# First products of the MLP in half of its pieces as eleven block products instead of twelve, with block sums made in place

## The chip, the cores and the metric

The kernel runs on one core of a Trainium2 chip. The metric is device time in microseconds, from one launch. In the profile's rows the core's engines are PE (TensorE; PEld is its loading of weights), DVE (VectorE), ACT (ScalarE), POOL (GpSimd) and SP (SyncE, which here only issues DMAs). SBUF holds 128 partitions; PSUM has eight banks, each 512 fp32 columns wide, into which TensorE accumulates and from which ACT and DVE read.

## The reference

Attention with a delta rule over q, k, v of shape 4 x 8 x 768 x 48, then a two-layer MLP over 3072 tokens. All arithmetic is fp32; w_in and w_out arrive as 64-bit floats and are narrowed on the chip.

```python
k_n = k / (norm(k) + 1e-6)
for t in range(768):                         # per batch b and head h
    y[t] = q[t] @ state
    state += beta[t] * outer(k_n[t], v[t] - k_n[t] @ state)
x = y.transpose(0, 2, 1, 3).reshape(3072, 384)
h = x @ w_in                                 # 384 x 2048
out = (h * sigmoid(h)) @ w_out               # 2048 x 384
```

## The kernel before

**Tiling.** The 768 tokens of a sequence are worked in six chunks c = 0 to 5 of 128 tokens (of all four batches and eight heads), each in two halves hf of 64 tokens. A half is 256 rows of x (4 batches x 64 tokens), kept transposed as xT: 3 blocks k of 128 features, 256 columns. There are thus twelve MLP halves (c, hf).

**The MLP of a half.** `hidden(c, hf)` makes the first product in eight steps f. Each step covers 256 of the 2048 hidden features: six matmuls of a 128x128 weight by 256 columns (j = 0, 1 and k = 0 to 2) fill one bank `phid` (L952), and one ScalarE activation (L962, Silu) of 128x512 moves it into a tile `gT`, which holds three steps (a group). An fp32 matmul appears in the trace as two records, so that a half has 96 of them. `combine(c, hf)` makes the second product for c > 0. It is done with a scheme of seven products of blocks: seven chains of eight matmuls 128x128 by 192 columns (L1050), accumulated in the banks `px` and `py`. Their left operands are blocks of gT or sums S1 to S4 of such blocks, made by VectorE (`sum_g`, L1032) into `sums_of_g`; their right operands are blocks of w_out or the three sums `sums_of_w`, made once. Results go into `o` by ScalarE (scaled by 0.5); three of them are first kept by ScalarE (`kept`, L1058) and added by VectorE (L1061). In the last half of the program VectorE adds the last one straight from PSUM (L1096). For chunk 0 `project` makes the second product plainly (L982).

**The attention.** For each chunk `prepare` makes scores (`pg` L408, `pa` L488, copied by ScalarE at L503 and masked by VectorE at L498), writes them to DRAM in another layout (`blocks`) and reads them back (`g`). `invert` then inverts triangular 32x32 blocks with 31 steps of two VectorE operations (L562, L567) and ends at L570; its results travel through DRAM again (`up`, `xi`, `xe`), and `merge` (L711) joins them. `solve` uses the result: `keys` (ph, L757), `inner` (pz, L769), `update` (pu, L789), `old` and `new` (pyc, L835 and L848). `new` copies its output into xT; what lies on other partitions goes through `part` and is moved by DMAs (`move`, L828).

**Order.** Every instruction's place on its engine is fixed: `pin` ties each operation behind the last one on the same engine, and `in_line` does so for SyncE's DMAs. The MLP is a stream of generator steps (`pieces`); the attention code calls `run(n)` at fixed places, which executes the next n steps. So a hand-written order interleaves the two on every engine. In chunk c's part of the loop, `solve(c)` runs with the MLP's steps left over from the chunk before; `feed_forward(c, 0)` and `feed_forward(c, 1)` are added to the stream at its step n == 6; then follow `prepare(c + 1)` and `invert(c + 1)`, where three of four steps of the inversion also run a step of the MLP:

```python
for n, _ in enumerate(invert(c + 1, step)):
    if n % 4 != 3:
        run()
```

Banks come from three pools: A and CC for the attention, M for the MLP. In chunk 0 `joins` (33 to 59 us) uses A and CC for the first merge.

Of the kernel before, what the change touches and what calls it, by code (L numbers as in the profile page):

```python
# [19 lines left out]
def kernel(  # L20
# [10 lines left out]
    nc = tc.nc  # L31
# [24 lines left out]
    mlp = ctx.enter_context(tc.tile_pool(name="mlp", bufs=2))  # L56
    psA = ctx.enter_context(tc.tile_pool(name="psA", bufs=3, space=PSUM))
    psC = ctx.enter_context(tc.tile_pool(name="psC", bufs=3, space=PSUM))
    psM = ctx.enter_context(tc.tile_pool(name="psM", bufs=2, space=PSUM))
    A, CC, M = (psA, "a"), (psC, "c"), (psM, "m")  # L60
# [98 lines left out]
    def in_blocks(c):  # L159

        return 1 < c < NCH
# [27 lines left out]
    states = [const.tile([P, HB, NP, W], FP32, name=f"state{g}") for g in range(2)]  # L189
    beta_fm = mlp.tile([BH, NCH, 2, W], FP32, name="beta_fm", tag="gT", bufs=3)  # L190
    for g in range(2):
# [65 lines left out]
    def fetch_w_in(i):  # L257
        if i in (0, 1, 6):
            raw = mlp.tile([P, SIZE], U32, name="raw", tag="gT", bufs=3)[:]
        elif i < 6:  # L260
            raw = room(i // 2 - 1, i % 2)
        else:
            raw = spare
        raw = raw.rearrange("p (a f) -> p a f", a=NKT)
        src = moe_w_in.rearrange("(a p) f -> p a f", p=P)[:, :, i * WF : (i + 1) * WF].bitcast(U32)
        in_line(nc.sync.dma_start(out=raw, in_=src))
        raws["in", i] = raw.rearrange("p a (f j) -> p a f j", j=2)
# [495 lines left out]

    def inner(c, g, hf, room=A):

# [60 lines left out]
    def move():  # L826
        for to, of in moves:
            in_line(nc.sync.dma_start(out=to, in_=of))  # L828
        moves.clear()

# [12 lines left out]
    def new(c, g, hf):  # L843
# [13 lines left out]
        for h in chained(range(1, H, 2), range(0, H, 2)):  # L857
            f = D * h
            while f < D * (h + 1):
# [4 lines left out]
                if h % 2 == 1:  # L864
                    if g == 1:
                        moves.append((
                            xT[f % P : f % P + n, f // P].rearrange("p (g t) -> p g t", g=2),
                            parts[c, hf][at : at + n, :, h // 2, :],
                        ))
                else:  # L870
                    by_act(to, py[at : at + n, C * (h // 2) : C * (h // 2 + 1)])
# [71 lines left out]
    gTs = {}  # L943

    def hidden(c, hf):

        for f in range(NFF // 2):
            assert ("in", f) in narrowed
            ph = bank(M, "phid")
            for j in range(2):  # L950
                for a in range(NKT):
# [3 lines left out]
                        rhs=xTs[c, hf][:, a, :],  # L955
                        start=(a == 0), stop=(a == NKT - 1),
                    ))
                if j == 0:
                    yield
            if f % FG == 0:  # L960
                gTs[f // FG] = mlp.tile([P, FG, 2 * GT], FP32, name="gT", bufs=3)
            pin(nc.scalar.activation(  # L962
                out=gTs[f // FG][:, f % FG, :], in_=ph[:], func=ACTF.Silu, scale=-0.5 if in_blocks(c) else 0.5
            ))
            if c > 0 and f % FG == 1 and f >= FG:
                for which in (S1, S2):
                    sum_g(which, f // FG - 1)
            yield
# [32 lines left out]
    def sum_w():  # L1001
# [14 lines left out]
    S1, S2, S3, S4 = (  # L1016
        (0, (0, 1), (1, 1), ALU.add), (1, 0, (0, 0), ALU.subtract),
        (0, (0, 0), (0, 1), ALU.subtract), (1, (1, 0), 1, ALU.subtract),
    )
# [3 lines left out]

    def sum_g(which, g):
        k, left, right, op = which
        fs = group(g)
        of = [
            sums_of_g[:, x, fs] if isinstance(x, int) else
            gTs[g][:, 0 : fs.stop - fs.start, x[0] * GT + x[1] * C : x[0] * GT + (x[1] + 1) * C]
            for x in (left, right)  # L1030
        ]
        pin(nc.vector.tensor_tensor(out=sums_of_g[:, k, fs], in0=of[0], in1=of[1], op=op))  # L1032

    NG = -(-NFF // 2 // FG)

    def combine(c, hf):

        o = mlp.tile([P, 2, DM], FP32, name="o", bufs=1)
        kept = mlp.tile([P, 3, HM], FP32, name="kept", bufs=1)
        px, py = bank(M, "px"), bank(M, "py")  # L1040
        left, right = slice(0, HM), slice(HM, DM)
        last = c == NCH - 1 and hf == 1

        def chain(to, a, b, start=False):
            for f in range(NFF // 2):
                if isinstance(a, int):
                    at = sums_of_g[:, a, f]
                else:
                    at = gTs[f // FG][:, f % FG, a[0] * GT + a[1] * C : a[0] * GT + (a[1] + 1) * C]
                pin(nc.tensor.matmul(  # L1050
# [5 lines left out]

        def keep(i, of):
            pin(nc.scalar.mul(kept[:, i], of, 0.5))  # L1058

        def add(to, of):  # L1060
            pin(nc.vector.tensor_tensor(out=to, in0=to, in1=of, op=ALU.add))  # L1061

        def steps(chain, *halfway):
            for n, _ in enumerate(chain):
                if n == 1:
                    break
                for which, g in halfway:
                    sum_g(which, g)
                yield

        yield from steps(chain(px[:, left], (0, 0), (0, 0), True), (S1, NG - 1), (S2, NG - 1))
        yield
        yield from steps(chain(px[:, right], (1, 1), 2))
        pin(nc.scalar.mul(o[:, :, left], px[:, 0:DM].rearrange("p (n m) -> p n m", n=2), 0.5))
        yield
        yield from steps(chain(py[:, left], 0, (0, 1), True))
        pin(nc.scalar.mul(o[:, 1, right], py[:, left], 0.5))
        yield
        yield from steps(chain(px[:, left], 1, 1), *((S3, g) for g in range(NG)))
        pin(nc.scalar.mul(o[:, 0, right], px[:, left], 0.5))  # L1080
        yield
        yield from steps(chain(py[:, right], (1, 0), (1, 0)), *((S4, g) for g in range(NG)))
        keep(0, py[:, right])
        if last:
            add(o[:, 0, left], kept[:, 0])
            store(c, hf, o, 0, left)
        yield
        yield from steps(chain(px[:, left], 0, 0))
        keep(1, px[:, left])
        add(o[:, 1].rearrange("p (n m) -> p n m", n=2), kept[:, 1].unsqueeze(1).to_broadcast([P, 2, HM]))  # L1090
        if last:
            store(c, hf, o, 1)
        yield
        yield from steps(chain(py[:, left], 1, (1, 1)))
        if last:
            pin(nc.vector.scalar_tensor_tensor(  # L1096
                out=o[:, 0, right], in0=py[:, left], scalar=0.5, in1=o[:, 0, right], op0=ALU.mult, op1=ALU.add
            ))
            store(c, hf, o, 0, right, True)
            yield  # L1100
            return
        keep(2, py[:, left])
        add(o[:, 0, right], kept[:, 2])
        add(o[:, 0, left], kept[:, 0])
        for n in range(2):
            store(c, hf, o, n)
        yield

    def feed_forward(c, hf):

        yield from hidden(c, hf)
        if c > 0:
# [293 lines left out]
    for c in range(1, NCH):  # L1406
        solving = solve(c)
        long = lengths(c + 1) if c + 1 < NCH else iter(())
        for n in range(10):
            go(solving)  # L1410
            run(2 if n == 6 else 0 if n == 5 and c == 1 else 1)
            if n == 6:
                if c == 1:
                    run(999)
                    needed = iter(())
                pieces = chained(pieces, feed_forward(c, 0), feed_forward(c, 1))
            go(long, (1, 1, 0, 1, 1, 9, 5, 5, 5, 5)[n])
# [51 lines left out]
```

## Time and profile before

| | us |
|---|---|
| runs | 674.14, 676.48, 677.03 |
| median | 676.48 |
| profiled execution | 676.0 |
| its span | 674.3 |
| PE busy, its granted clock | 647.6, 0.984 |
| ACT busy | 218.6 |
| POOL busy | 84.3 |

The profiled execution is 1.7 us longer than the span of its instructions and 0.5 us below the median. A row of the page reads: line, engine, operation, output<-inputs, shape, count | busy time, mean ns of one | idle time of the engine just before these instructions, and what ended most of it. Matmuls are pipelined: a record's duration is longer than the spacing of records. A row of the chain or the timeline reads: start, duration, engine, group of instructions.

### The profile page before, as it was taken

How to read it: one execution, taken by the hardware profiler on the slowest of the kernel's cores; microseconds unless marked ns; L12 is line 12 of the kernel's file. 1: busy time of each engine (PE TensorE's matmuls, PEld its weight loads, DVE VectorE, ACT ScalarE, POOL GpSimd, SP SyncE). 2: the span in 40 equal slices, each digit the busy share in tenths (PEclk: the TensorE clock that was granted, in tenths of full speed). 3: DMA queues.
4: the chain of work that ended last, by engine and by line, in shares of the span. 5: the costliest groups of instructions: out<-in, count | busy, mean ns of one | idle time of the engine just before them, and what ended most of it. 6: DMA issues, size and time to landing. Idle time of an engine off the chain costs nothing.

```text
span 674.3 us, 20956 instructions
## 1 busy us (share of the span) xinstructions
PE 647.6 (96%) x9288; PEld 566.1 (84%) x9288; DVE 388.4 (58%) x883; ACT 218.6 (32%) x504; POOL 84.3 (13%) x86
## 2 busy tenths in 40 slices
PE   8849998899999999999999999999999999999997
PEld 5548885586688989988989988989888989989997
DVE  5846687994463892573982574973564972312112
ACT  2436675022343122443122442122442132431111
POOL 5022384400102000102000002001002000000000
PEclk9967999999999999999999999999999999999999
DMA  9891628505072904076814076624073023010101
GB/s 131 207 265 61 216 97 178 102 0 107 10 154 46 153 23 96 13 125 129 110 35 85 15 141 128 90 50 72 15 154 76 1 70 50 17 36 1 24 0 24
DMA packets 146906, 55.72 MB, mean 83 GB/s; under 512 B 118192, under 2 KB 139952, under 8 KB 146816
## 3 DMA queue, kind: packets, MB, share of 16 engines
q1 hardware_dynamic: 144624, 54.07, 40.7%
q8 instruction: 73, 1.20, 0.8%
q10 hardware_dynamic: 2192, 0.31, 0.3%
q14 instruction: 17, 0.14, 0.1%
HBM read 40.40 MB, written 11.80 MB: 77 GB/s over the span
## 4 chain that ended last, share of the span: by engine, by line
PE 75%; DVE 4%; DMA 3%; ACT 1%; issue 1%; SPq 1%; POOL 0%; ACTq 0%; DVEq 0%
PE phid L952 31%; PE px L1050 15%; PE py L1050 12%; PE po L982 4%; PE pa L488 2%; PE pz L769 2%; PE pu L789 2%; PE px L711 2%; PE py L711 2%; PE ph L757 2%; PE pyc L835 1%; PE pyc L848 1%; DVE rank L562 1%; DMA sums_of_w<-in_moe_w_out_dram 1%; DVE x L567 1%
## 5 line engine op out<-in xcount | busy, mean ns | idle before, releaser
L952 PE MATMUL phid<-xT,w_in 128*128 128x256 f32 x1152 | 257.2, 382 | 0.0
L952 PEld LDWEIGHTS phid<-xT,w_in 128*128 128x128 f32 x1152 | 216.3, 190 | 31.4 <-issue 1.9
L962 ACT ACTIVATE gT<-phid 128x512 f32<-128x512 f32 x96 | 57.4, 598 | 159.3 <-PE phid L952 153.1
L1032 DVE TENSOR_TENSOR sums_of_g<-gT 128x384 f32<-128x384 f32 (+1 forms) x60 | 29.2, 509 | 79.8 <-ACT gT L962 69.5
L562 DVE SCALAR_TENSOR_TENSOR rank<-g,step,x 128x31 f32<-128x31 f32 (+15 forms) x155 | 63.8, 412 | 17.7 <-DMA g<-blocks 13.2
L1050 PE MATMUL py<-w_out,sums_of_g 128*128 128x192 f32 x320 | 58.2, 331 | 0.0
L567 DVE TENSOR_TENSOR x<-x,rank 128x31 f32<-128x31 f32 (+15 forms) x155 | 54.7, 353 | 5.4
L1050 PE MATMUL px<-sums_of_w,sums_of_g 128*128 128x192 f32 x320 | 57.2, 330 | 0.0
L1050 PEld LDWEIGHTS px<-sums_of_w,sums_of_g 128*128 128x128 f32 x320 | 52.0, 190 | 0.8
L1050 PEld LDWEIGHTS py<-w_out,sums_of_g 128*128 128x128 f32 x320 | 51.9, 190 | 0.8
L982 PE MATMUL po<-w_out,gT 128*128 128x384 f32 x128 | 44.3, 495 | 5.1 <-POOL w_out L221 2.5
L351 POOL TENSOR_TENSOR sq<-kb 128x384 f32<-128x384 f32 x24 | 21.1, 898 | 223.4 <-PE px L711 217.4
L982 PEld LDWEIGHTS po<-w_out,gT 128*128 128x128 f32 x128 | 23.4, 190 | 20.9 <-POOL w_out L221 3.1
L450 DVE STREAM_TRANSPOSE kq<-stage 128x512 f32<-128x512 f32 x28 | 28.5, 1101 | 11.6 <-DMA stage<-in_q_dram 9.1
L503 ACT COPY xT<-pyc 48x128 f32<-48x128 f32 x132 | 34.2, 259 | 1.7
L769 PEld LDWEIGHTS pz<-vf,xi 64*64 64x64 f32 x768 | 27.4, 141 | 6.2 <-issue 4.8
L430 POOL TENSOR_TENSOR vf<-vf,n_slot 128x768 f32<-128x768 f32 x10 | 15.6, 1577 | 129.7 <-DMA vf<-in_v_dram 97.2
L769 PE MATMUL pz<-vf,xi 64*64 64x48 f32 x768 | 30.3, 227 | 1.3 <-issue 1.2
L498 DVE TENSOR_TENSOR ap<-pa,above 128x256 f32<-128x256 f32 x44 | 16.6, 419 | 22.8 <-ACT ap L503 21.8
L1061 DVE TENSOR_TENSOR o<-o,kept 128x192 f32<-128x192 f32 (+1 forms) x29 | 11.5, 421 | 31.5 <-ACT kept L1058 31.3
L1050 PE MATMUL py<-w_out,gT 128*128 128x192 f32 x160 | 29.1, 331 | 0.0
L1050 PE MATMUL px<-w_out,gT 128*128 128x192 f32 x160 | 27.6, 326 | 0.0
(172 smaller groups left out, 855.6 us busy)
## 6 DMA issues: line engine op xcount, KB each, us to landing
vf<-in_v_dram SPq DMA_DIRECT2D x24, 192.0 KB, 4.6
out_dram<-o SPq DMA_DIRECT2D x46, 96.0 KB, 2.2
sums_of_w<-in_moe_w_out_dram SPq DMA_DIRECT2D x5, 768.0 KB, 5.9
w_out<-in_moe_w_in_dram SPq DMA_DIRECT2D x4, 768.0 KB, 7.1
blocks<-ap SPq DMA_DIRECT2D x44, 64.0 KB, 1.9
g<-blocks SPq DMA_DIRECT2D x5, 512.0 KB, 3.6
up<-x SPq DMA_DIRECT2D x5, 512.0 KB, 4.0
xi<-up SPq DMA_DIRECT2D x20, 128.0 KB, 3.9
```

What stands on the lines that cost most here:

```text
L351: pin(nc.gpsimd.tensor_tensor(out=squared[c, b // HB][:, b % HB], in0=kb, in1=kb, op=ALU.mult))
L450: pin(nc.vector.transpose(out=kqs[c, b][:, :, j, :].rearrange("p a (i m) -> p a m i", i=T), in_=src.rearrange("p a (m d) -> p a m d", d=D) ...
L503: return pin(nc.scalar.copy(to, of))
L562: pin(nc.vector.scalar_tensor_tensor(out=tv, in0=g[:, 0:m, m : m + 1].to_broadcast([P, m, n]), scalar=step[:, m : m + 1], in1=x[:, m : m + ...
L567: yield pin(nc.vector.tensor_tensor(out=x[:, 0:m, m:T], in0=x[:, 0:m, m:T], in1=tv, op=ALU.add))
L711: yield pin(nc.tensor.matmul(pm[to, T * n : T * (n + 1)], lhsT=left, rhs=right, start=True, stop=True))
L769: yield pin(nc.tensor.matmul(pz[rows, n * D : (n + 1) * D], lhsT=xis[g][rows, u * H + 2 * p + e, :], rhs=vfs[c][rows, hf, g * HB + u, p, : ...
L952: pin(nc.tensor.matmul(ph[:, j * GT : (j + 1) * GT], lhsT=w_in[:, a, (2 * f + j) * P : (2 * f + j + 1) * P], rhs=xTs[c, hf][:, a, :], star ...
L962: pin(nc.scalar.activation(out=gTs[f // FG][:, f % FG, :], in_=ph[:], func=ACTF.Silu, scale=-0.5 if in_blocks(c) else 0.5))
L982: pin(nc.tensor.matmul(po[n][:, 0:DM], lhsT=gTs[f // 2 // FG][:, f // 2 % FG, at : at + C], rhs=w_outs[f // HFF][:, f % HFF, :], start=(f ...
L1032: pin(nc.vector.tensor_tensor(out=sums_of_g[:, k, fs], in0=of[0], in1=of[1], op=op))
L1050: pin(nc.tensor.matmul(to, lhsT=at, rhs=quarter(f, *b) if isinstance(b, tuple) else sums_of_w[b][:, f], start=start and f == 0, stop=f == ...
```

## The change

Six of the twelve halves, `FAST`, make the first product differently: (1,0), (2,0), (3,0), (4,0), (5,0) and (5,1). There `hidden_fast` treats the two weight columns i, the two halves n of the 256 columns and the blocks k = 0 and 1 as a product of 2x2 blocks, which needs seven block products in place of eight; k = 2 adds four plain ones. That is eleven matmuls of 128x128 by 128 columns per f instead of six by 256, which are twelve such blocks.

The scheme needs sums of weight blocks, s1 to s4 for each f, made once by GpSimd (`supply`: six f's in chunk 1 at n == 6, the others later); sums of x, t3, t2, t4 and one in place in xT, made by GpSimd at the start of each FAST half; and partial results, which are copied out of the bank by ScalarE (`begin_pair`: 128x256, `sixth`: 128x128, `seventh`: 128x128), added by VectorE (128x128 and, from PSUM, 128x384) and then activated (128x128 and 128x384). sixth and seventh write the same quarter of the bank, one after the other has been copied away.

All of gT is now one buffer, `gbuf`, which also takes the weights' and x's sums. The sums S1 to S4 are made in place in gT, for every half. So they must wait for the matmuls that read what they overwrite: S1 of the first two groups stays in hidden, S2 moves into combine, and S3 and S4 come later in it. px and py are added into o by VectorE straight from PSUM where the next half is FAST, and otherwise through ScalarE's copy, which now also holds for the last half of the program. `ahead_of_time` starts the next half, where it is FAST, within the combine before it (three of its steps). `late` marks (5,0), whose next half is FAST as well: there S4 is made in another block. The banks are A 2, CC 2, M 4, where they were 3, 3, 2; `inner` uses CC. Staging of beta and of some raw w_in moves into gbuf.

The core of the diff:

```diff
-    psA = ctx.enter_context(tc.tile_pool(name="psA", bufs=3, space=PSUM))
-    psC = ctx.enter_context(tc.tile_pool(name="psC", bufs=3, space=PSUM))
-    psM = ctx.enter_context(tc.tile_pool(name="psM", bufs=2, space=PSUM))
+    psA = ctx.enter_context(tc.tile_pool(name="psA", bufs=2, space=PSUM))
+    psC = ctx.enter_context(tc.tile_pool(name="psC", bufs=2, space=PSUM))
+    psM = ctx.enter_context(tc.tile_pool(name="psM", bufs=4, space=PSUM))
...
-    def inner(c, g, hf, room=A):
+    def inner(c, g, hf, room=CC):
...
+    def supply():
+        f = supplied[0]
+        supplied[0] += 1
+        if f >= NFF // 2:
+            return
+        s1, s2, s3, s4 = homes[4 * f : 4 * f + 4]
+        minus(s1, block_of(f, 1, 0), block_of(f, 1, 1), ALU.add, by=nc.gpsimd)
+        minus(s2, s1, block_of(f, 0, 0), by=nc.gpsimd)
+        minus(s3, block_of(f, 0, 0), block_of(f, 1, 0), by=nc.gpsimd)
+        minus(s4, block_of(f, 0, 1), s2, by=nc.gpsimd)
+
+    def hidden_fast(c, hf):
+        x = [[xTs[c, hf][:, k, n * C : (n + 1) * C] for n in range(2)] for k in range(NKT)]
+        t3, t2, t4 = (t_sums[:, i] for i in range(3))
+        minus(t3, x[1][1], x[0][1], by=nc.gpsimd)
+        minus(x[0][1], x[0][1], x[0][0], by=nc.gpsimd)
+        minus(t2, x[1][1], x[0][1], by=nc.gpsimd)
+        minus(t4, x[1][0], t2, by=nc.gpsimd)
...
+        def begin_pair(f):
+            phs[f] = bank(M, "phid")
+            times(at(f, 1, 0), block_of(f, 0, 0), x[0][0], True)
+            times(at(f, 1, 1), homes[4 * f], x[0][1])
...
+            pin(nc.scalar.copy(g_of(f)[:, 1:3], quarters_of(f)[:, 0:4:3]))
+
+        def sixth(f):
+            times(at(f, 1, 0), homes[4 * f + 1], t2)
+            pin(nc.scalar.copy(g_of(f)[:, 0], quarters_of(f)[:, 0]))
+            to = g_of(f)[:, 2]
+            minus(to, to, g_of(f)[:, 0], ALU.add)
+
+        def seventh(f):
+            times(at(f, 1, 0), homes[4 * f + 2], t3)
+            pin(nc.scalar.copy(g_of(f)[:, 3], quarters_of(f)[:, 0]))
+
+        def others(f, some):
+            for n in some:
+                times(*(
+                    (at(f, 0, 1), homes[4 * f + 3], x[1][1]),
+                    (at(f, 0, 1), block_of(f, 0, 2), x[2][1], False, True),
+                    (at(f, 0, 0), block_of(f, 0, 2), x[2][0]),
+                    (at(f, 0, 0), block_of(f, 0, 1), x[1][0], False, True),
+                    (at(f, 1, 1), block_of(f, 1, 2), x[2][1], False, True),
+                    (at(f, 1, 0), block_of(f, 1, 2), x[2][0]),
+                    (at(f, 1, 0), block_of(f, 1, 1), t4, False, True),
+                )[n])
+                if n == 0:
+                    supply()
+            if n == 6:
+                silu(g_of(f)[:, 0], quarters_of(f)[:, 0])
+                minus(g_of(f)[:, 1:4], quarters_of(f)[:, 1:4], g_of(f)[:, 1:4], ALU.add)
...
+        def last_of(f):
+            silu(g_of(f)[:, 1:4], g_of(f)[:, 1:4])
+            if f % FG == 1 and f >= FG:
+                sum_g(S1, c, hf, f // FG - 1)
+
+        for f in range(n):
+            sixth(f)
+            if f > 0:
+                others(f - 1, range(2))
+            if f + 1 < n:
+                begin_pair(f + 1)
+            yield
+            if f > 0:
+                others(f - 1, range(2, 4))
+            seventh(f)
+            if f > 0:
+                others(f - 1, range(4, 7))
+            if f > 1:
+                last_of(f - 2)
+            yield
...
     S1, S2, S3, S4 = (
-        (0, (0, 1), (1, 1), ALU.add), (1, 0, (0, 0), ALU.subtract),
-        (0, (0, 0), (0, 1), ALU.subtract), (1, (1, 0), 1, ALU.subtract),
+        ((0, 1), (0, 1), (1, 1), ALU.add), ((0, 0), (0, 1), (0, 0), ALU.subtract),
+        ((1, 1), (1, 1), (0, 0), ALU.subtract), (None, (1, 0), (0, 0), ALU.subtract),
     )
...
+        then = (c, 1) if hf == 0 else (c + 1, 0)
+        late = (c, hf) in FAST and then in FAST
+        first = (1, 0) if late else (0, 0)
...
+        kept = None if then in FAST else gbuf[:, AT_SUMS : AT_SUMS + 2 * HM].rearrange("p (i m) -> p i m", i=2)
+
+        def add(to, of, i, both=False):
+            if kept is None:
+                of = of.unsqueeze(1).to_broadcast([P, 2, HM]) if both else of
+                pin(nc.vector.scalar_tensor_tensor(
+                    out=to, in0=of, scalar=0.5, in1=to, op0=ALU.mult, op1=ALU.add
+                ))
+                return
             pin(nc.scalar.mul(kept[:, i], of, 0.5))
...
+        def ahead_of_time():
+            if then in placed and then in FAST:
+                go(ahead(*then))
...
+        yield from first_half(chain(px[:, left], (0, 0), (0, 0), True), (S1, NG - 1))
         yield
+        yield from first_half(chain(px[:, right], (1, 1), 2), (S2, 0))
         pin(nc.scalar.mul(o[:, :, left], px[:, 0:DM].rearrange("p (n m) -> p n m", n=2), 0.5))
+        yield from second_half((S2, 1))
+        yield from first_half(chain(py[:, left], (0, 1), (0, 1), True), (S2, 2))
         pin(nc.scalar.mul(o[:, 1, right], py[:, left], 0.5))
+        yield from second_half((S3, 0))
+        yield from first_half(chain(px[:, left], (0, 0), 1), (S3, 1))
         pin(nc.scalar.mul(o[:, 0, right], px[:, left], 0.5))
+        ahead_of_time()
+        yield from second_half((S3, 2))
+        yield from first_half(chain(py[:, right], (1, 0), (1, 0)), *(() if late else [(S4, 0)]))
+        add(o[:, 0, left], py[:, right], 0)
...
+        yield from second_half(*(() if late else [(S4, 1)]))
+        for n, _ in enumerate(chain(px[:, left], (1, 1), 0)):
+            if n == 0:
+                for g in range(NG) if late else [2]:
+                    sum_g(S4, c, hf, g, first)
+                ahead_of_time()
+                yield
+        add(o[:, 1].rearrange("p (n m) -> p n m", n=2), px[:, left], 1, True)
...
+        for n, _ in enumerate(chain(py[:, left], first, (1, 1))):
...
+        add(o[:, 0, right], py[:, left], 0)
```

## The prediction

> **What bounds the kernel now.** I read the page's first and fourth parts (busy time by engine, and the chain that ended last by engine), then that chain in order of time: start, us, engine, group.
>
> ```profile
> PE 647.6 (96%) x9288; PEld 566.1 (84%) x9288; DVE 388.4 (58%) x883; ACT 218.6 (32%) x504; POOL 84.3 (13%) x86
> ...
> PE 75%; DVE 4%; DMA 3%; ACT 1%; issue 1%; SPq 1%; POOL 0%; ACTq 0%; DVEq 0%
> ```
>
> ```profile
> 418.69 5.20 PE px L1050 x32
> ...
> 436.89 20.72 PE phid L952 x96
> 457.61 5.20 PE px L1050 x32
> 462.81 2.14 PE py L711 x128
> ...
> 592.74 20.92 PE phid L952 x96
> ...
> 631.86 20.72 PE phid L952 x96
> ...
> 670.82 0.36 DVE o L1096
> ```
>
> TensorE is busy 96% of the span and carries 75% of the chain, so its stream is what has to get shorter. One undisturbed half of the first product is 96 records in 20.72 us, 216 ns each. Between the first halves of chunks 2, 3 and 4 the chain has starts at 293.39, 393.43 and 493.46, a period of 100.0 us; a microsecond saved per chunk counts only if the period shortens. Then the rows of the instructions the change uses:
>
> ```profile
> L952 PE MATMUL phid<-xT,w_in 128*128 128x256 f32 x1152 | 257.2, 382 | 0.0
> L952 PEld LDWEIGHTS phid<-xT,w_in 128*128 128x128 f32 x1152 | 216.3, 190 | 31.4 <-issue 1.9 <-ACT o L987 0.6
> L962 ACT ACTIVATE gT<-phid 128x512 f32<-128x512 f32 x96 | 57.4, 598 | 159.3 <-PE phid L952 153.1 <-DVE rank L562 6.1
> L503 ACT COPY ap<-pa 128x256 f32<-128x256 f32 x48 | 15.7, 378 | 15.5 <-PE pa L488 14.3 <-DVE ap L506 1.2
> L1032 DVE TENSOR_TENSOR sums_of_g<-gT 128x384 f32<-128x384 f32 x40 | 21.5, 553 | 52.2 <-ACT gT L962 42.2 <-PE py L1050 10.0
> ```
>
> ```profile
> 194.40 1.91 PE L462 MATMUL pt<-ident,kb 128*128 128x128 f32 x16
> ```
>
> The last is from the timeline: 16 full-array records of 128 columns, each with its own 128x128 load, lie in 1.91 us. With 0.273 us for the last one alone (that tile's median) the spacing is (1.91 - 0.273)/15 = 109 ns.
>
> **The change, part by part.** 1. *The products.* A FAST half issues per f eleven 128-column matmuls, two records each: 176 in all in place of 96 of 256 columns. At 109 ns that is 19.18 us against 20.73: a gain of 1.55 us a half, 9.3 us in six. For the load I have a second row: at 302.49 us a 32-column record stands alone behind a 128x128 load, and raw starts put its stream about 110 ns after that load began; at 112 ns a record the gain is 1.0 us a half, 6.1 in all. I take 109, measured on the same shape. The range keeps 6.1.
>
> 2. *ScalarE.* Per f one activation of 512 becomes copies of 256, 128 and 128 and activations of 128 and 384. Rows give 0.38 us for 256 columns, 0.48 for 384 (the copy of z) and 0.60 for 512, so I estimate 0.27 for 128: 0.38 + 3 x 0.27 + 0.49 = 1.7 us where it was 0.6, against 2.4 us of TensorE per f. ACT has the room, 68% idle, but it is no longer only behind TensorE: sixth's copy must be done before seventh writes the same quarter of the bank, and six matmuls (12 x 0.109 = 1.31 us) lie between. Undisturbed, the chain is 0.27 to end the last record, 0.04 to ACT, 0.27 copy, 0.05 back: it fits, also with a 0.38 copy ahead. Cost in chunk 5: 0.
>
> 3. *VectorE.* Per f an add of 128 columns (0.2 us estimated) and one of 384 from PSUM (0.47 start to start): 5.4 us a half more. Sums S1 to S4 keep their number, but S2 of the first two groups moves from the hidden half, where DVE has idle time, into combine. There DVE is nearly full, because the 31 steps of the inversion lie in the same in-order queue:
>
> ```profile
> 418.79 0.27 DVE L562 SCALAR_TENSOR_TENSOR rank<-g,step,x 128x31 f32<-128x31 f32 x1 [3.46 <-DMA g<-blocks]
> ...
> 425.96 1.35 DVE L1032 TENSOR_TENSOR sums_of_g<-gT 128x384 f32<-128x384 f32 x3
> ...
> 428.94 1.35 DVE L1032 TENSOR_TENSOR sums_of_g<-gT,sums_of_g 128x384 f32<-128x384 f32 x3
> ...
> 434.69 0.56 DVE L1061 TENSOR_TENSOR o<-o,kept 128x384 f32<-128x384 f32 x1 [0.67 <-ACT kept L1058]
> ```
>
> The inversion begins when g lands at 418.8, and that is set by SyncE, whose issues run without a break from 390.7 to 413.1, not by TensorE. In the combine from 318.7 to 336.9 DVE is busy 16.27 of 18.20 us. Now two more S2 sums (2 x 0.47) and, because TensorE comes about 1.5 us earlier to the same point, the adds of f = 6 and 7 (2 x 0.67) fall behind that start as well: 16.27 + 0.94 + 1.34 = 18.55 us. In the new order the sums S4 stand last. Adding the queue's entries ahead of S4's second group from the rows gives some 18.9 us after the inversion's start; the seventh chain needs it 16.6 us after hidden ends, which is 1.2 to 2.0 us later than the inversion starts. TensorE waits 0.3 to 1.1 us; I take 0.7 in each of chunks 2, 3 and 4. Behind that wait stand combine's last matmuls, the next half and the merge.
>
> 4. *The merge behind it.* The merge at L711 needs an exchange that landed about 1.9 us before TensorE came to it (460.9 against 462.8). The inversion now ends 0.5 to 1.2 us later and TensorE comes up to 1.3 earlier: about even. Cost 0, up to 0.6 a chunk in the range.
>
> 5. *Chunk 1.* Its FAST half must wait for the transfers of xT and four POOL sums behind them, where before TensorE filled such gaps (L982, L952) between attention pieces; one step of that stretch now issues no matmul at all. I estimate 1.6 us idle. The inversion starts 3.7 us behind the end of hidden there in the trace (221.20 against 217.50), so S4 is later too: 2.6 us, of which 1.6 is the same idle time counted twice. Cost 2.6 (ends 1.6 and 4.2). The weight sums are 32 POOL operations of some 0.4 us (0.83 for 384 columns, 1.48 for 768, hence the estimate), 13 us on an engine busy 13%: hidden by its idle time, unless they run ahead of the x sums; that is in the upper end.
>
> 6. *Banks, and sums straight from PSUM.* A and CC have two banks each, not three, M four. The chunk before the period is where A's third bank matters: joins(0), 33 to 59 us, takes its banks one stage later. TensorE idles there mostly on issue, so 0.4 us, ends 0 and 1.5. In the attention pieces later, adjacent pieces still alternate banks: 0.2 us in each of chunks 2, 3, 4. Adding px and py into o without ACT's kept copy removes 0.33 us from an idle path: nothing. Only the last add of the program is the other way round: ACT 0.33 and a wake-up of 0.04 come ahead of the DVE add that at 670.82 read PSUM itself. Nothing runs beside it: +0.4 us.
>
> Sum: chunk 5: -3.1 + 0.4 = -2.7; chunks 2 to 4: 3 x (-1.55 + 0.7 + 0.2) = -1.95; chunk 1: -1.55 + 2.6 = +1.05; start: +0.4. Together -3.2 us, from 9.3 that TensorE saves. Against the profiled execution's 676.0 that is 672.8; the median of the runs is 0.5 higher, so 676.48 - 3.2 = 673.3. A difference under 0.5%, 3.4 us, a measurement of this kernel hardly tells from no change.
>
> **The rivals.** *A. Most of it is kept.* If the S4 wait is nothing (the inversion leaves gaps of 0.67 us at 434 that I did not hand out) and chunk 1 loses only 1.6: -9.3 + 0.4 + 1.6 + 0.4 = -6.9, or 669.6. For: 75% of the chain is TensorE. Against: DVE's 16.27 of 18.20.
>
> *B. All of it is eaten.* With 112 ns a record, 1.1 us of wait in each of three chunks, 0.6 at the merge, 2.6 in chunk 1: -6.1 + 3.3 + 1.8 + 2.6 + 0.8 + 0.6 = +3.0, or 679.5; midway between this and the sum lies 676, no change.
>
> *C. Slower: ACT and DVE hand the bank to and fro, and TensorE waits in the hidden half.* Before, a hidden half gives ACT one operation per f with 1.99 us idle ahead of it. Now ACT's activation of the first quarter waits for DVE's small add, and ACT's next copies queue behind it. In the half that starts at 393.4, DVE's queue holds transposes in two bursts of 2.05 us (398.0, 401.1) and masks in two of 1.63 (404.3, 409.0), and ACT holds 2.2 us of copies (393.5 to 395.8). If each holds a step for all but the 1.31 us of cover: 2 x 0.74 + 2 x 0.32 + 0.9 = 3.0 us a chunk, four times: 673.3 + 12 = 685.3. It decides when a burst lasts longer than the distance to the next use of the quarter. Against: the small add is issued nearly a whole f (2.4 us) ahead of the activation that needs it, which covers the bursts of 2.05. I expect a third of it at most.
>
> *D. The load paces the record.* If 128 columns cannot hide a 128x128 load (mean 190 ns in the row), the records go at the shortest spacing that matmuls of this kernel with such loads show, 163 ns at 192 columns: 28.7 us a half, +8.0, six times: 724. The 16 transposes at 109 ns speak against it, though their loads are recorded at 142 ns, not 190.
> The Trainium skill, "TensorE: Matmul & The Clock Gate", section "Back-to-back issue gap", says that in a stream of loads and matmuls both set the spacing, 81 ns for 128 columns where streaming alone takes 56; scaled by that ratio, 109 would become an estimated 158 ns and the time would be near 718. The trace's transposes do not agree with it.
>
> **How the numbers follow.** The sum's own case (671 to 676): 0.42, about half of it below 673.1. A: 0.22. B: 0.14, nearly all within 0.5%. C, 680 and above: 0.18. D: 0.04. Faster 0.22 + 0.20 = 0.42; same 0.35, slower 0.23. The range reaches from A's 669.6 with 1 us more for a start without loss, 668.5, up to 682, which takes in the lower part of C; above it lie the rest of C and D, below it little.
>
> **What would show it.** Hidden halves of chunk 5 at 19.2 us (D: 28; C would not show there). In chunks 2 to 4 a wait of px or py at L1193, the last chain, for DVE's sums, 0.3 to 1.1 us, and a period of 98.9 to 99.6 us. In chunk 1 TensorE idle on POOL's x sums around 190 us. An ACT operation ahead of the last DVE add. Wrong would be: idle time of TensorE inside FAST halves behind ACT copies (C), or a period of 98.5 and less (A).

## The result, and the profile after

The changed kernel takes 680.50 us (median of six runs, 678.91 to 684.45); the kernel before, beside it, 676.56 (six runs, 674.14 to 677.98). The ratio is 1.0068, 95% interval 1.0043 to 1.0093: slower by about 4 us, where 3.2 us less were forecast. The profiled execution took 680.65 us, its span is 678.8 (before 674.3).

The page's busy times and the chain by engine, of the changed kernel:

```profile
PE 651.5 (96%) x9768; PEld 581.3 (86%) x9768; DVE 425.1 (63%) x979; ACT 259.6 (38%) x682; POOL 108.8 (16%) x142
...
PE 73%; DVE 13%; ACT 4%; DMA 4%; issue 3%; SPq 2%; POOL 1%; ACTq 0%; DVEq 0%; POOLq 0%
```

TensorE's busy time did not fall, and DVE's share of the chain rose from 4% to 13%. The chain in order of time shows where:

```profile
134.51 20.72 PE phid L1095 x96
...
341.79 20.72 PE phid L1095 x96
...
410.37 12.57 PE phid L1008 x110
439.75 2.10 PE py L1193 x10
441.85 20.72 PE phid L1095 x96
...
638.32 18.44 PE phid L1008 x162
```

The first row is the half (0,1). The chain of the kernel before has it at

```profile
129.95 20.92 PE phid L952 x96
```

So some 4.5 us are lost before any FAST half has run (4.56 by the chain, 4.46 by the starts of the records themselves, which the table below takes). Between 410.37 + 12.57 = 422.94 and 439.75 the chain leaves TensorE for VectorE, and comes back for the last ten records of the seventh chain: the wait for S4. The half that follows starts at 441.85, and the one a chunk earlier at 341.79: a period of 100.06 against 100.03 before (436.89 - 336.86). The last row is the undisturbed FAST half (5,1).

How far the changed kernel is behind, by the starts of the same piece of work in the two traces:

| up to | behind by, us | in this stretch |
|---|---|---|
| start of half (0,1) | 4.46 | +4.46 |
| start of (1,1) | 5.72 | +1.26 |
| start of (2,1) | 4.94 | -0.78 |
| start of (3,1) | 4.96 | +0.02 |
| start of (4,1) | 5.44 | +0.48 |
| end of hidden (5,0) | 4.77 | -0.67 |
| end of hidden (5,1) | 4.19 | -0.58 |
| end of the span | 4.5 | +0.3 |

The spans are known to 0.1 us.

The rows of the instructions, groups with their shapes kept apart:

```profile
L1008 PE MATMUL phid<-xT,w_in 128*128 128x128 f32 x576 | 87.8, 277 | 0.0
L1008 PEld LDWEIGHTS phid<-xT,w_in 128*128 128x128 f32 x576 | 75.6, 192 | 1.4 <-issue 1.4
L1020 ACT COPY gT<-phid 128x128 f32<-128x128 f32 x48 | 12.5, 260 | 5.5 <-PE phid L1008 5.5
L974 DVE TENSOR_TENSOR gT<-gT 128x128 f32<-128x128 f32 x48 | 16.1, 335 | 7.1 <-ACT gT L1020 6.1
L1046 ACT ACTIVATE gT<-gT 128x384 f32<-128x384 f32 x48 | 24.9, 518 | 5.9 <-DVE gT L974 5.8
```

ScalarE's copies of 128 columns take 0.26 us, where 0.27 was estimated. The records of the FAST halves follow one another nearly without idle time: in the half (5,0) the spacing of successive starts is 109 to 112 ns in 170 of 173 cases, each load beginning 2 or 3 ns behind the start of the record before. The three others are 407, 213 and 195 ns. The longest of them comes once a half, at its first f, and is a wait for ScalarE's copy of `seventh` (engine, line waited for: us in all, times, longest):

```profile
PEld phid L1008 <- ACT gT L1026: 1.9, 6, 0.3
```

### The profile page after: what moved, and what is told of

Read it like the earlier page. It is cut to its first block, busy times and chain, and to the rows that moved or that the text cites. A ratio compares the mean times of both kernels' runs of the same rounds, so it can differ in the third digit from the quotient of the medians.

```text
span 678.8 us, 22299 instructions
## 1 busy us (share of the span) xinstructions
PE 651.5 (96%) x9768; PEld 581.3 (86%) x9768; DVE 425.1 (63%) x979; ACT 259.6 (38%) x682; POOL 108.8 (16%) x142
## 3 DMA queue, kind: packets, MB, share of 16 engines
q8 instruction: 77, 1.26, 0.8%
## 4 chain that ended last, share of the span: by engine, by line
PE 73%; DVE 13%; ACT 4%; DMA 4%; issue 3%; SPq 2%; POOL 1%; ACTq 0%; DVEq 0%; POOLq 0%
PE phid L1008 16%; PE phid L1095 15%; PE px L1193 9%; PE py L1193 8%; DVE rank L569 4%; DVE x L574 4%; PE po L1124 4%; PE pa L495 3%; PE pz L776 3%; DVE gT L1175 3%; PE pw L325 2%; PE pu L796 2%; PE ph L764 2%; PE py L718 2%; PE px L718 2%
## 5 line engine op out<-in xcount | busy, mean ns | idle before, releaser
L1095 PE MATMUL phid<-xT,w_in 128*128 128x256 f32 x576 | 131.4, 387 | 0.0
L1095 PEld LDWEIGHTS phid<-xT,w_in 128*128 128x128 f32 x576 | 110.3, 193 | 15.7 <-issue 0.2
L1193 PE MATMUL py<-w_out,gT 128*128 128x192 f32 x480 | 87.7, 330 | 1.1 <-DVE gT L1175 1.1
L1008 PE MATMUL phid<-xT,w_in 128*128 128x128 f32 x576 | 87.8, 277 | 0.0
L1193 PE MATMUL px<-sums_of_w,gT 128*128 128x192 f32 x480 | 87.5, 331 | 0.0
L1175 DVE TENSOR_TENSOR gT<-gT 128x384 f32<-128x384 f32 (+1 forms) x120 | 61.6, 526 | 38.5 <-ACT gT L1105 33.1
L1193 PEld LDWEIGHTS py<-w_out,gT 128*128 128x128 f32 x480 | 78.1, 190 | 3.6 <-DVE gT L1175 2.7
L1193 PEld LDWEIGHTS px<-sums_of_w,gT 128*128 128x128 f32 x480 | 77.8, 190 | 1.4
L1008 PEld LDWEIGHTS phid<-xT,w_in 128*128 128x128 f32 x576 | 75.6, 192 | 1.4 <-issue 1.4
L974 DVE TENSOR_TENSOR gT<-phid,gT 128x384 f32<-128x384 f32 x48 | 26.7, 557 | 58.4 <-ACT gT L1046 58.4
L1105 ACT ACTIVATE gT<-phid 128x512 f32<-128x512 f32 x48 | 28.7, 598 | 71.1 <-PE phid L1095 68.9
```

Source lines behind the costliest of these rows:

```text
L974: return pin(by.tensor_tensor(out=to, in0=left, in1=right, op=op))
L1008: pin(nc.tensor.matmul(to, lhsT=left, rhs=right, start=start, stop=stop, skip_group_check=True))
L1095: pin(nc.tensor.matmul(ph[:, j * GT : (j + 1) * GT], lhsT=w_in[:, a, (2 * f + j) * P : (2 * f + j + 1) * P], rhs=xTs[c, hf][:, a, :], star ...
L1105: pin(nc.scalar.activation(out=gTs[f // FG][:, f % FG, :], in_=ph[:], func=ACTF.Silu, scale=-0.5 if in_blocks(c) else 0.5))
L1175: pin(nc.vector.tensor_tensor(out=to, in0=left, in1=right, op=op))
L1193: pin(nc.tensor.matmul(to, lhsT=at, rhs=quarter(f, *b) if isinstance(b, tuple) else sums_of_w[b][:, f], start=start and f == 0, stop=f == ...
```

## The experiments

Ratios are to the kernel before, on the same chip. The profiled starts of the half (0,1) spread from 128.8 to 132.1 us over nine kernels whose start has three banks in A, so single spans are compared from there on only. In the four kernels with two banks in A it begins between 134.1 and 136.8.

**1. The banks alone.** The kernel before, and

```diff
-psA bufs=3, psC bufs=3, psM bufs=2;  inner(..., room=A)
+psA bufs=2, psC bufs=2, psM bufs=4;  inner(..., room=CC)
```

> The kernel before with only the PSUM banks of the change (A 2, CC 2, M 4; inner in CC). Theory 1 (the change's start is late because A and CC lost a bank each): the half (0,1) begins at 134 us instead of 129.9 and the total is +4, near 680.5. Rival (the start is late because of gbuf: staging of w_in and beta in it): 129.9 and 676.5, as before.

681.08 us, ratio 1.0075 (1.0049 to 1.0102): the whole loss of the change, without any part of its arithmetic. Half (0,1) begins at 134.09, and the period behind it is 100.04: the fewer banks cost the start and nothing later.

**2. The change with the old banks in the start.** The eight banks are 2 + 2 + 2 and two single ones, which belong to A and CC until the loop over chunks begins, and to M from there:

```diff
+    rings = {"a": [psA, psA, psX[0]], "c": [psC, psC, psX[1]], "m": [psM, psM]}
+    def later_banks():
+        rings.update({"a": [psA, psA], "c": [psC, psC], "m": [psM, psM, *psX]})
...
+    later_banks()
     for c in range(1, NCH):
```

> The changed kernel with the old division of the eight banks (3, 3, 2) until chunk 1's loop begins, and 2, 2, 4 from there. Theory 1: the half (0,1) begins at 130 us again and the total falls by 4.2, to 676.3, as before the change. Rival (gbuf): 134.3 and 680.5.

675.76 us, ratio 1.0003 (0.9989 to 1.0017), and the half (0,1) begins at 129.24 in the chain. The start is repaired and the loss is gone; what is left of the change is no gain. The rival, gbuf, falls.

**3. No FAST half.**

```diff
-FAST = [(c, hf) for c in range(1, NCH) for hf in range(2) if hf == 0 or c == NCH - 1]
+FAST = []
```

> The changed kernel with no FAST half: all twelve halves by six matmuls of 256 columns; banks, gbuf and sums in place stay. If the eleven products gain some 0.6 us in each half of chunk 5 and lose 1.5 in chunk 1 as the two traces suggest, this is 680.5 - 1.5 + 1.2 + (0 to 1) = 680.2 to 681.2, the combine's last chain waits less than 0.3 us for VectorE and the period is 100.0. Rival (the FAST halves themselves are what costs): 677 or less. Rival (sums in place cost by themselves): the last chain waits 0.7 us here too, 682.

680.67 us, ratio 1.0069 (1.0044 to 1.0094). In the chain the halves (2,1) and (3,1) start at 342.27 and 442.31, a period of 100.04, and no chain waits: the sums in place cost nothing by themselves. From the half (0,1) to the end of the span its profiled execution takes 543.0 us (679.8 - 136.78), the changed kernel 544.3 (678.8 - 134.51): in these two executions the six FAST halves lose 1.3 us. By stages, from half to half, no_fast takes 105.2 us to (1,1) and 100.3, 100.0 and 100.0 to the next three, the changed kernel 106.9, 100.4, 100.1 and 100.5; in chunk 5 the FAST halves gain 0.4 and 0.6. So chunk 2's -0.78 in the table above is not theirs: the kernel without them has it too. banks_alone takes 105.9 and 101.2 for the first two stages, so the gain there belongs to what else the change brings, the sums in place among it; which part is not tried.

**4. Plain products with 128 columns.** The kernel before, each matmul split in two:

```diff
-rhs=xTs[c, hf][:, a, :]
+for n in range(2): ... rhs=xTs[c, hf][:, a, n * C : (n + 1) * C]
```

> The kernel before with each matmul of 256 columns as two of 128 with a weight load of their own, nothing else changed: 192 records a half. If a 128-column record is paced by its load at 111.7 ns, as in the changed kernel's trace, a half takes 21.45 us (before 20.73) and the total is +8 us, 685. Rival (the 111.7 came from the waits around ACT and DVE, and alone it is 109, as for the transposes): 20.93 a half, +2.4, 679.

685.63 us, from a single run, so the total has no interval. From the chain of this kernel, one half:

```profile
442.59 21.44 PE phid L953 x192
```

21.44 us for 192 records is 111.7 ns each, with ACT and DVE as they were. So the pace is that of 128-column records with a load each, and not of the waits around them.

**5. S3 on GpSimd.** start_banks, and

```diff
+by = nc.gpsimd if which is S3 and (c, hf) in FAST and c < NCH - 1 else nc.vector
-pin(nc.vector.tensor_tensor(out=to, in0=left, in1=right, op=op))
+pin(by.tensor_tensor(out=to, in0=left, in1=right, op=op))
```

> start_banks with the three sums S3 of the FAST halves of chunks 1 to 4 made by GpSimd instead of VectorE. Theory 2 (in chunks 2 to 4 VectorE's in-order queue, with the inversion's steps in it, is late with S4 and the last chain of combine waits 0.7 us for it): the wait goes, the period falls from 100.05 to about 99.35, and the total by 2.1, to 673.6. Rival (the queue is not what is late; the sums wait for TensorE's reads or for GpSimd's 0.83 us an operation): the last chain still takes 3.3 us and the total stays at 675.8. Rival (the wait goes but the merge then waits for the inversion): chain 2.60, period still 100.05, TensorE idle at the merge L728.

681.68 us, ratio 1.0075 (1.0056 to 1.0094): worse than start_banks by some 5 us, going by the ratios. Period 100.92 (343.49 to 444.41 in the chain), and the last chain takes 4.1 us, not 2.6. None of the three expectations holds, and the timelines of GpSimd and of VectorE in this kernel show why the last chain is late:

```profile
429.78 1.01 POOL L1188 TENSOR_TENSOR gT<-gT 128x384 f32<-128x384 f32 x1 [17.37 <-DVE gT L1188]
432.52 1.05 POOL L1188 TENSOR_TENSOR gT<-gT 128x384 f32<-128x384 f32 x1 [1.73 <-PE py L1206]
```

```profile
429.52 0.41 DVE L579 SCALAR_TENSOR_TENSOR rank<-g,step,x 128x192 f32<-128x192 f32 x1
429.97 1.03 DVE L584 TENSOR_TENSOR x<-x,rank 128x192 f32<-128x192 f32 x1
...
431.51 0.37 DVE L584 TENSOR_TENSOR x<-x,rank 128x207 f32<-128x207 f32 x1
...
432.74 1.07 DVE L584 TENSOR_TENSOR x<-x,rank 128x220 f32<-128x220 f32 x1
```

The VectorE operation that comes up while GpSimd runs ends 0.2 us behind GpSimd's end: 1.03 and 1.07 us, where the one between them takes 0.37. Three such operations (the third takes 0.81 where the step behind it takes 0.41) last 1.8 us longer together, which is more than VectorE saved by handing over three sums of 0.55, 0.55 and 0.42 us, partly overlapped. The last ten records of the last chain begin 17.8 us after `combine` does (442.31 - 424.47), in start_banks 17.0 (433.62 - 416.65). This speaks for theory 2 from the other side: the later VectorE is, the longer the last chain. The Trainium skill, "SBUF — State Buffer", section "SBUF: two separate sides", says that a VectorE instruction with two SBUF inputs and a GpSimd instruction that reads SBUF hold a shared pair of ports by an exclusive lock, so that the one that comes second waits for the whole of the other. These rows agree in the main: 0.2 us is less than the 0.37 of a whole operation, but the profile's times of GpSimd are rough.

The periods account for 1.8 us of the loss. More of it lies ahead of them, in chunks 1 and 2 (107.6 and 103.6 us, in start_banks 106.05 and 100.3). In chunk 2 TensorE waits 0.9 us at the merge for the inversion's transfer, and behind that the granted clock falls to half (columns: window, length, busy us of PE, PEld, DVE, ACT, POOL; granted clock, DMA share, GB/s):

```profile
262.00:264.00 2.00, 1.11 (x66) 1.03 (x66) 0.00 (x0) 0.00 (x0) 0.00 (x0) 1.00 1.19 149
...
266.00:268.00 2.00, 2.00 (x9) 1.56 (x8) 0.52 (x1) 0.00 (x0) 0.00 (x0) 0.50 0.00 0
```

In start_banks it stays at 1.00 there. The rest of what chunks 1 and 2 lose was not taken apart.

**6. Without the FAST half of chunk 1.** start_banks, and (1,0) left out of FAST.

> start_banks with the half (1,0) made by six matmuls of 256 columns again. Theory 3 (the FAST half of chunk 1 loses more to its gaps around GpSimd's x sums and the weight sums than its 1.07 us): from the start of half (0,1) to that of half (1,1) 105.65 us as before the change, in place of 106.05, and the total 0.4 lower, 675.4. Rival (those gaps come from the attention's own waits): no change or +1.0, 676.8.

680.78 us, ratio 1.0069 (1.0049 to 1.0088). From half (0,1) to (1,1) it is 105.6 as theory 3 has it, but the 104.2 us from there to (2,1) are 3.9 more than in start_banks (100.3), so the total says nothing on theory 3. A plain half has 16 steps where a FAST one has 19, and everything behind it moved by three steps against the attention. TensorE's longest wait in chunk 2 is 1.8 us, inside the FAST half (2,0), for a copy of ScalarE's (L1031, that of `sixth`); the two periods behind are long as well, 100.9 and 100.8 us.

**7. The three mends together**: S3 on GpSimd, (1,0) plain, and the last sum straight from PSUM.

> start_banks with S3 on GpSimd, without the FAST half (1,0), and with the program's last sum made by VectorE straight from PSUM. If the three losses add: 675.8 - 2.1 - 0.4 - 0.35 = 672.9, below the kernel before by 0.4%. Rival (what the last chain no longer waits for is waited for at the merge): 675.0.

682.33 us, ratio 1.0081 (1.0057 to 1.0106). With mends 5 and 6 both failures, so is their sum.

**8. S4 earlier in VectorE's queue.** start_banks, and

```diff
-                if n % 4 != 3:
+                if n % 4 != 3 or n in (11, 15):
                     run()
...
-            run(8 if c == 1 else 10)
+            run(6 if c == 1 else 8)
```

> start_banks with two MLP steps moved from behind the inversion to its 12th and 16th step (and two fewer behind it), so that VectorE's queue has the sums S4 two inversion steps, 1.8 us, further ahead; no operation is added, taken or moved to another engine. Theory 2 (the last chain waits because S4 stands behind too many inversion steps): the last chain 2.60 us instead of 3.31 in chunks 2 to 4, period 99.3 to 99.7, total 674.2 or less. Rival (VectorE simply has more work than the stretch, so that the order does not matter): the wait reappears at the merge L728, period 100.0, total 675.8.

674.43 us, ratio 0.9994 (0.9977 to 1.0010). The chain of start_banks and then that of this kernel, at the same piece of work:

```profile
433.62 2.10 PE py L1204 x10
```

```profile
434.34 2.60 PE py L1204 x16
436.94 20.72 PE phid L1106 x96
```

In start_banks the chain comes from VectorE into the last ten records; here all 16 follow one another in 2.60 us, and the period is 99.34 (337.60 to 436.94). Theory 2 holds for the wait: it is the order of the queue, and the merges of chunks 3 and 4 take their 2.14 us without a wait. The merge of chunk 2 does wait here, 0.7 us for the inversion's transfer `xe`, as the rival said, and from (0,1) to (2,1) this kernel takes 207.1 us where start_banks takes 206.3. So of the 1.4 us that the two later periods gain half is lost again, and the total misses the 674.2 that was expected by 0.2. From the half (0,1) to the end of the span the profiled execution takes 542.4 us (672.8 - 130.44), 2.0 less than before the change (674.3 - 129.95 = 544.4); in the medians of whole runs that is within the interval.

**9. Theory 3 once more**, with three steps fewer ahead of chunk 2:

```diff
-            run(8 if c == 1 else 10)
+            run(5 if c == 1 else 10)
```

> start_banks without the FAST half (1,0), as in without_first, but with three MLP steps fewer ahead of chunk 2 (5 instead of 8), since a plain half has 16 steps and the FAST one 19: the half (2,0) then begins at the same place of the attention as in start_banks. Theory 3a (without_first lost its 3 to 4 us in chunk 2 because (2,0) began three steps too early, before the attention's copies on ScalarE were done): chunk 2 takes 100.3 to 101 us from half (1,1) to half (2,1) as in start_banks, total 675.4. Rival 3b (it lost them because the last weight sums were not ready): chunk 2 still takes 103 us or more, total 679 to 681.

684.11 us, ratio 1.0131 (1.0109 to 1.0152). Neither: chunk 2 takes 108.9 us. TensorE reached the merge before the inversion's transfers had landed and stood idle for 2.5 us up to 261.6, and after two records for 0.5 us more. Its chain and then its windows (columns as in 5):

```profile
254.94 3.99 DMA up<-x
...
259.36 3.02 DMA xe<-low
```

```profile
259.00:266.00 7.00, 3.97 (x130) 3.70 (x129) 0.70 (x1) 0.58 (x1) 0.00 (x0) 0.66 0.89 115
266.00:276.00 10.00, 10.00 (x177) 9.17 (x178) 3.75 (x6) 1.73 (x3) 2.05 (x3) 0.55 0.01 2
276.00:286.00 10.00, 10.00 (x297) 9.08 (x294) 4.91 (x12) 3.90 (x11) 1.18 (x2) 1.00 0.02 5
```

Behind that idle time the granted clock is 0.55 to 0.66 in the mean of these windows (0.50 from 262 to 274 in windows of 4 us). The same merge takes 4.4 us from its first record, the 0.5 us of waiting included, and 2.3 in start_banks.

**10. The last sum straight from PSUM**, on top of sums_earlier.

```diff
-kept = None if then in FAST else gbuf[...]
+kept = None if then in FAST or last else gbuf[...]
```

> sums_earlier with the program's last sum made by VectorE straight from PSUM as in the kernel before. If the 0.33 us copy on ScalarE stands alone on the path at the end: 0.3 to 0.4 us below sums_earlier. Rival: no difference, because the store that it releases waits for an earlier store.

675.13 us, ratio 0.9999 (0.9983 to 1.0016): not to be told from sums_earlier. From the last matmul record's start to the end of the span it is 3.90 us against 4.19, so ScalarE's copy does stand on the path, at 0.3 us, which the whole runs cannot resolve.

**11 and 12. Which bank.** start_banks with the third bank for CC only, and for A only, in the start:

```diff
-    rings = {"a": [psA, psA, psX[0]], "c": [psC, psC, psX[1]], "m": [psM, psM]}
+    rings = {"a": [psA, psA], "c": [psC, psC, psX[1]], "m": [psM, psM, psX[0]]}     # start_cc3
+    rings = {"a": [psA, psA, psX[0]], "c": [psC, psC], "m": [psM, psM, psX[1]]}     # start_a3
```

> start_banks with only CC given its third bank in the start (A 2, CC 3, M 3; inner in CC). If the start's 4.2 us come from the idle-filling matmuls pw and the second half of the scores, which rotate through CC: the start is whole again, half (0,1) at about 130 us, total 676. If they come from A (scores, beta, pyc held until ScalarE has copied xT): 133 to 134 us, total 679.5. If both hold: 132, 677.5.

> start_banks with only A given its third bank in the start (A 3, CC 2, M 3; inner in A). The mirror of start_cc3: if A is what held it, 130 us and 676; if CC, 133 to 134 us and 679.5; if both, 132 and 677.5.

CC only: 681.15 us, ratio 1.0080 (1.0050 to 1.0110), half (0,1) at 136.40. A only: 675.93 us, ratio 1.0017 (0.9993 to 1.0041), half (0,1) at 130.50. So it is A and not CC. (`inner` goes with A's third bank in both kernels, so the two are not separated; but start_cc3 is late at the joins already, 38.7 us against 34.1 in start_banks, and `inner` first runs some 16 us later.) The windows from 60 to 80 us of the changed kernel, and then of start_a3:

```profile
60.00:80.00 20.00, 18.58 (x493) 15.22 (x494) 13.68 (x21) 12.25 (x23) 5.53 (x3) 0.87 0.34 101
```

```profile
60.00:80.00 20.00, 19.45 (x510) 16.22 (x512) 14.49 (x23) 13.38 (x25) 7.96 (x5) 1.00 0.58 200
```

With two banks in A the transfers of this stretch, the weights' among them, move at 101 GB/s instead of 200, and in the 20 us behind it at 181 instead of 87: they are issued later. The granted clock is 0.87 as well, not 1.00.

**13. Chunk 1's half plain, its steps kept.** sums_earlier_tail with (1,0) out of FAST and three empty steps ahead of it:

```diff
+        if (c, hf) == (1, 0):
+            for _ in range(3):
+                yield
+            supply()
+            supply()
```

> sums_earlier_tail with the half (1,0) by matmuls of 256 columns, but with three empty steps ahead so that it has the FAST half's 19 steps and nothing behind it moves in the order; the last weight sums are made in it. If the FAST half of chunk 1 loses more than it gains: from half (0,1) to half (1,1) 105.7 us instead of 106.0 to 106.8, chunk 2 as in sums_earlier (100.1 to 100.3), total 674.4. Rival (the empty steps cost TensorE the same idle time, since they fall into the same gaps): 106.6 or more and 675.1 as sums_earlier_tail.

675.96 us, ratio 1.0002 (0.9981 to 1.0023). From half (0,1) to (1,1) 107.2 us, not fewer than the 106.6 of sums_earlier_tail. The rival holds: with the plain half and no empty steps the stretch takes 105.6 us (without_first) or 106.05 (without_first_2), with them 107.2, so what chunk 1 loses is mostly the steps without a matmul. Whether the FAST half gains 0.6 us in them is open: with the same FAST half the stretch takes 106.05 us in start_banks and 106.75 in start_a3. Theory 3 falls in this form. Chunk 2 takes 101.6 us, not the 100.1 to 100.3 that were expected: there too a wait at the merge (0.5 us) is followed by a granted clock of 0.50, from 264 to 266.

## Why the prediction was wrong

**The banks (step 6) are the term that failed.** It put the third bank of A at 0.4 us, ends 0 and 1.5, by looking at the joins alone, where TensorE idles on issue. The loss is 4.46 us up to the half (0,1). banks_alone shows that the banks make all of it that can be measured, start_cc3 and start_a3 that it is A's bank (with `inner`, which goes with it) and not CC's. It begins ahead of the joins: TensorE reaches them at 36.3 us, not 33.1. Among the waits of TensorE's weight loads from 8 to 36 us in the changed kernel is one that all four kernels with two banks in A have (0.9 to 1.0 us), and the kernel before, start_banks and start_a3 do not:

```profile
PEld pb L338 <- ACT ap L510: 0.9, 1, 0.9
```

From 90 to 134 us the scores wait for banks whose pyc ScalarE is still copying into xT:

```profile
PE pa L495 <- ACT xT L510: 2.3, 2, 1.5
```

But TensorE waits longer in that stretch of the kernel before (5.1 us, all of it at L982). What decides when (0,1) begins is there, in both chains, a load of w_out, whose data go through ScalarE, VectorE and GpSimd before the po ahead of the half can start. In the kernel before and then in the changed one:

```profile
105.34 6.17 DMA sums_of_w<-in_moe_w_out_dram
```

```profile
109.27 6.79 DMA sums_of_w<-in_moe_w_out_dram
```

In all four kernels with two banks in A it starts between 109.3 and 111.4 us, in start_banks and start_a3 at 103.2 and 104.2, and the half follows 24.6 to 26.7 us later in all seven. Ahead of it in the chain stand, with two banks, ScalarE's copies and SyncE's issues of the attention; before, VectorE's work. How the lost time grows from the joins to this load (banks_alone is only 1.7 us late at the joins) is read from these rows and the windows, and not tried by itself. The step failed in its method: a bank is a resource of every stage that rotates through the pool, and only one stage was costed. The other two parts of the step were right or nearly so. The 0.2 us a chunk for the attention later is 0 (period 100.04 in banks_alone). The tail's 0.4 measured 0.35: VectorE's last add begins 3.16 us behind the last chain's first record, where it was 2.81.

**The products (step 1) were mis-sized.** 109 ns was taken from the transposes, with the row behind pg giving 112 as the other bound. It is 111.7, in the change and in plain128, so that the undisturbed gain is 20.73 - 176 x 0.1117 = 1.07 us a half, not 1.55. Of that the halves (5,0) and (5,1) show 0.67 and 0.58 against the kernel before; banks_alone and no_fast are 0.28 us shorter up to the end of (5,0) as well, so that the FAST half's own share there is 0.4. Gaps of 0.3, 0.1 and 0.1 us between the records of each half make most of the rest. The transposes' loads are recorded at 142 ns, and the matmuls' at 192; the prediction had that difference in hand under rival D and used it only against 163. The longer load may make the 3 ns, but no run changes the load alone. The Trainium skill, "TensorE: Matmul & The Clock Gate", section "LDWEIGHTS (loading the stationary operand)", gives columns / 1.2 ns, 107 for 128: the spacing found is 5 ns above that. The ratio taken from its section "Back-to-back issue gap" (an estimated 158 ns) is not borne out.

**The wait for S4 (step 3) was right in place, cause and size.** 0.7 us was forecast; the last chain takes 3.32 us in chunks 2 and 3, 3.74 in chunk 4, against 2.60: waits of 0.7, 0.7 and 1.1. sums_earlier shows that it is the queue's order. But with 1.07 us to start from, 0.4 of it lost to gaps and to the switching around the scores, nothing was left, and the period did not move. The forecast of 98.9 to 99.6 holds for the mended kernel alone (99.34).

**The merge (step 4)** costs nothing in chunks 3 and 4, as forecast. **Chunk 1 (step 5)** was forecast at +1.05 and measures +1.26 (+1.7 against no_fast), but not by the wait that was named: TensorE is idle for 2.8 us from 176 to 206 us, where the kernel before has 0.8 from 172 to 202, and the waits recorded there are for ScalarE's z and xT and VectorE's vf, none for GpSimd's sums of x. **ScalarE (step 2)** was put at 0 and measures 0.3 us a FAST half: the step checked the way from `sixth`'s copy to `seventh`; the wait that comes is behind `seventh`'s copy, at the first f, where no matmuls of an f before lie in between. So rival C's mechanism is there in small: six waits of 0.3 us, 1.9 us in all, where C asked for 3 us a chunk. Rival B gave 679.5, near the measured 680.5, but by other terms: it too had the start at 0.4.

Taken together: forecast -3.2, measured +4.5 in the profiled executions. Of the 7.7 between them the start makes 4.1, chunk 5's products 1.85 (-3.1 forecast, -1.25 measured), and chunks 2 to 4 1.7 (-1.95 and -0.28); chunk 1 and the tail the 0.1 that is left. The -0.28 is flattered by chunk 2, whose -0.78 no_fast has without a FAST half. That the forecast's range of 668.5 to 682 holds the measured 680.5 is due to the rivals that it made room for, and not to the sum.

## What to carry to other kernels

When a change takes banks from one pool for another, cost it in every stage that rotates through that pool, the start too, which lost 4.5 us here while the later chunks lost nothing; making that change alone (the pools' sizes and `inner`'s pool in the kernel before) would have shown it in one run. A finer blocking of a product pays only by the spacing of records at the new width, which should be measured on matmuls (111.7 ns here) and not on transposes (109). And in an in-order queue a sum's place is worth as much as its duration: two steps moved removed a wait that another engine's help made longer.

## What the runs showed that was not expected

- A VectorE add that meets a GpSimd add lasts until that one ends: 1.03 and 1.07 us instead of 0.37 (s3_on_pool). GpSimd's own adds of 128x384 took 1.0 us.
- In without_first_2 an idle stretch of 2.5 us on TensorE, and 0.5 more behind two records, was followed by some 14 us at a granted clock of 0.55 to 0.66. By the chain that cost 5.5 us (3.62 + 2.86 + 3.56 + 2.75 us for merges and chains that otherwise take 2.14 + 1.50 + 2.14 + 1.50). The Trainium skill, "TensorE: Matmul & The Clock Gate", section "HAM oscillation — how this bites in real kernels", warns of idle gaps above some 3.4 us; here shorter ones were enough. In s3_on_pool a wait of 0.9 us at the merge was followed by 0.50 from 266 to 268 us, in first_same_steps one of 0.5 us by 0.50 from 264 to 266. In sums_earlier a wait of 0.7 us at the same place left the clock at 1.00, so the length of the wait alone does not decide it; what does is not shown.
- None of the thirteen kernels beats the kernel before by more than its interval. The best, sums_earlier, is at 0.9994 (0.9977 to 1.0010), though its trace is 2.0 us shorter behind the start.
